# First mixture: weights split ahead of the branch, weight buffers taken in another order, rows by one queue

## The chip, the cores and the metric

The kernel runs on one core of a Trainium2 chip. The metric is the device time of one execution in microseconds; lower is better.

## The reference, cut to what matters

Causal attention with 64-row blocks, then a mixture in which a row goes to at most one of eight experts (the first mixture), then a mixture in which every row goes through all four experts (the second). The change lies in the first mixture.

```python
def _moe_ref(x, w_skip, w_gate, w1, w2):          # N, D, E, F = 2304, 512, 8, 1024
    do_compute = x @ w_skip > 0
    out = x.copy()
    xc = x[do_compute]
    logits = xc @ w_gate
    e_idx = np.argmax(logits, axis=1)
    # gate_w: the softmax weight of the chosen expert
    for e in range(E):
        mask = e_idx == e
        h = np.maximum(xc[mask] @ w1[e], 0.0)
        y[mask] = gate_w[mask, None] * (h @ w2[e])
    out[do_compute] = xc + y
```

With the inputs of the run 807 of 2304 rows go to an expert: 7, 9, 127, 179, 459, 16, 2 and 8 rows for experts 0 to 7.

## The kernel before, in words

**Stages.** Attention is computed in tiles of at most 128 query rows; each finished tile x is stored to the array XN and, once its expert is known, scattered by POOL into a second array XS, in which every expert has a region of its own (`route`, L480). `counts` (L491) then works out how many tiles each expert needs. `m1` (L848) is the first mixture, `m2` (L1141) the second; `m2` reads XN, which `m1` has updated in place.

**The first mixture** goes through its experts in four pairs, 0 and 1, 2 and 3, 4 and 5, 6 and 7; here they are pairs 0 to 3. A pair has two parts.

1. `m1_pair` (L790) handles the first 32 rows of both experts. Its matmuls take the weights in float32 as they were loaded: `hb` (x times w1, L807), a transpose `tb` (L799), `yb` (h times w2, L823). Those rows are in one tile xa, loaded from XS once (L864).
2. Rows beyond 32 are done in tiles of 128 rows, `more` and `m1_tile`, nested conditionals at L914: tile t of a pair runs if `alls[i] > t`. These tiles use weights split into a high and a low part, `wh` and `wl` (`w_split`, L699: a copy on ACT, a subtraction on DVE). `turnb` tells at which tile the pair's second expert begins; its split is inside a conditional at L933 (L927 where the first expert has no tile). In this run pair 1 has three tiles (one of expert 2, two of expert 3), pair 2 has four (all of expert 4), pairs 0 and 3 have none.

In pairs 1 to 3 two of the first expert's eight pieces are split ahead of the conditional, by `cut` within `m1_pair`; the other six are split inside the first tile, `split(0, ...)` under `tc.If(turnb[i] > 0)` at L924.

**The weights** come from memory in pieces of 512 KB, eight per expert (four of w1, then four of w2 once both w1 are in), 16 per pair, 64 in all, plus four first pieces of the second mixture. The list `plan` (consts, L136) fixes their order; here they are loads 0 to 67. Loads 0 to 15 belong to pair 0, 16 to 31 to pair 1, 32 to 47 to pair 2; pair 3 has 48 to 56 and 61 to 67, and loads 57 to 60 are the second mixture's.

Every load goes into a buffer (a room): 7 of kind s, 4 of kind d, 8 of kind r, 2 of kind e, 21 in all; `RM` (L64) gives a kind for each load, and rooms of a kind are taken in turn. `fetch` (L780) issues loads on SP's queue as far as the room's former holder belongs to a pair whose code has been written; it is called during attention's end, twice at the start of `m1` and after each pair. SP works its queue in order, so a load that has to wait for its room holds all loads behind it. SP takes no part in the conditionals; a room whose last reader stands inside a conditional is free for SP when the engines have passed that conditional.

At the start of `m1`, SP issues loads 11 to 14, then half of xa, then loads 15 to 20; ACT issues the other half of xa. `alls` and `turnb` are read into registers (L889, L890) after the first transposes of xa. `hint` (L883) tells PE, ACT and DVE ahead of time which way the branch at L914 will go; it stands behind `m1_x` in `m1_pair`.

```python
            if k not in self.rooms or len(past) >= room and past[-room] >= self.done1:
                return
```

Of the kernel before, what the change touches and what calls it, by code (L numbers as in the profile page):

```python
# [6 lines left out]
F32 = mybir.dt.float32  # L7
# [47 lines left out]
class Kernel:  # L55
# [2 lines left out]
    PTB = 1  # L58
    TLAG = 2
    RB = 7  # L60
    R3 = 4, 8, 2
    FL = 3
    RM = "s" * 7 + "r" + "d" * 4 + "r" * 7 + "e" * 2 + "s" * 4 + "d" * 4 + "s" * 3 + "r" * 8 + "e" + "d" * 3 + "e" + "s" * 7 \
        + "r" * 4 + "e" + "d" * 4 + "r" * 4 + "e" + "s" * 2  # L64
    CM = 6
    XO = 0
    S0 = "Aa02Bb13...V.vXx"
# [50 lines left out]
    def consts(self, cp, ac):  # L118
        nc, self.cp = self.nc, cp
        self.ident = cp.tile([128, 128], F32, name="ident")  # L120
        make_identity(nc, self.ident)
        self.minus = cp.tile([128, 128], F32, name="minus")

        self.maskl = ac.tile([128, 128], F32R, name="maskl")
        self.maskr = ac.tile([128, 64], F32R, name="maskr")
        nc.vector.memset(self.maskl.bitcast(F32), 0.0)
        nc.vector.memset(self.maskr.bitcast(F32), 1.0)
        self.mask4 = ac.tile([128, 128], F32R, name="mask4")
        nc.vector.memset(self.mask4.bitcast(F32), 0.0)
# [9 lines left out]
        self.plan = [(*x, k) for x, k in zip(plan[:57] + first + plan[57:], self.RM)]  # L139
        self.size = dict(s=self.RB, d=self.R3[0], r=self.R3[1], e=self.R3[2])  # L140
        self.raws, self.done1, self.stored = {}, 0, 0
        self.rooms, self.held = dict(s=self.ws), {k: [] for k in self.size}
# [347 lines left out]
    def counts(self):  # L490
# [7 lines left out]
        V.tensor_copy(self.own, t)  # L498
        V.tensor_copy(n, self.own)
        nA, nB = (n.rearrange("p (i o) -> p i o", o=2)[:, :, o] for o in range(2))  # L500
        V.tensor_tensor(t[:, 0:4], nA, nB, ALU.add)
        V.tensor_copy(self.alls, t[:, 0:4])
        V.tensor_scalar(end, tot[:, 0:8], -128.0, 0.0, ALU.add, ALU.max)
# [179 lines left out]

        return self.ws.tile([128, 20 * D], F32, tag="raw", name=name)[:, 0:n]

    def w_raw(self, w, i, e, c, pool=None):

        cols = slice(c * 256, (c + 1) * 256)
        r = pool.tile([128, 1024], F32, tag="raw", name=f"r{i + 1}") if pool else self.raw(1024, f"r{i + 1}")
# [91 lines left out]
    def fetch(self, n=99):  # L781

        for _ in range(min(n, len(self.plan) - len(self.raws))):
            p, x, k = self.plan[len(self.raws)]
            past, room = self.held[k], self.size[k]
            if k not in self.rooms or len(past) >= room and past[-room] >= self.done1:
                return
            past.append(p)
            self.raws[x[0] is self.w21 or x[0] is self.w22, *x[1:]] = self.w_raw(*x, pool=None if k == "s" else self.rooms[k])

    def m1_pair(self, xT, raws, cut, x, room, hint, before):

# [3 lines left out]
        def turn(i):  # L796
            tp = self.ps_t.tile([128, 2, 128], F32, tag="t", name="tb")
            for c in range(2):
                nc.tensor.transpose(tp[:, c], hs[i][:, c * 128:(c + 1) * 128], self.ident)  # L799
            hT.append(wk.tile([128, 2, 128], F32, tag=f"hT{i}", bufs=1, name="hT"))  # L800
            nc.scalar.copy(hT[i], tp)

        for i, raw in enumerate(raws):
            hp = self.ps_h.tile([128, 256], F32, tag="h", name="hb")
            for k in range(4):
                for j in range(4):
                    nc.tensor.matmul(hp[32 * j:32 * j + 32], lhsT=xT[i](k),  # L807
                                     rhs=raw[2 * (j // 2) + k // 2][:, k % 2, j % 2 * 256:j % 2 * 256 + 256],
                                     start=(k == 0), stop=(k == 3))
            cut()  # L810
            hs.append(wk.tile([128, 256], F32, tag=f"hs{i}", bufs=1, name="hs"))
            nc.scalar.activation(hs[i], hp, AF.Relu)
        turn(0)
        before()
        turn(1)
        x = self.m1_x(x, room)
        hint()
        cut()
        for i, raw in enumerate(raws):
            yps.append(self.ps_y.tile([128, 512], F32, tag=f"y{i}", name="yb"))  # L820
# [6 lines left out]
    def m1_join(self, i, yps):  # L827
# [7 lines left out]
        def out():  # L835
            p = slice(0, 64)
            x = self.xa[:, i]
            sm = self.ps_t.tile([128, 512], F32, tag="t", name="ysum")
            for o in range(2):
                nc.tensor.matmul(sm[32 * o:32 * o + 32], lhsT=self.sel, rhs=ys[o], start=True, stop=True)  # L840
            y = wk.tile([128, 512], F32, tag="sy", bufs=1, name="ys")
            nc.vector.scalar_tensor_tensor(y[p], sm[p], x[:, DM + 1:RW], x[:, 0:DM], ALU.mult, ALU.add)
            nc.gpsimd.indirect_dma_start(out=self.XN, out_offset=bass.IndirectOffsetOnAxis(
                ap=x[:, DM:DM + 1].bitcast(I32), axis=0), in_=y[p], in_offset=None, bounds_check=N - 1, oob_is_err=False)
        return out

    def m1(self):
# [10 lines left out]
            at = nc.values_load(self.row[0:1, i, t:t + 1], engines=pool, min_val=2 * i * N, max_val=2 * i * N + 2 * N - 128)  # L858
            return self.m1_load(bass.ds(at, 128), "xq", 2, nc.gpsimd, xg=xg)

        self.fetch(4)
        for i, q in enumerate((nc.sync, nc.scalar)):
            self.scat = list(scat)
            self.m1_load(None, q=q, xg=self.xa[ROWS * i:ROWS * i + ROWS], src=XE[i::2, 0:ROWS, :].rearrange("e n w -> n e w"))  # L864
        self.scat = list(scat)
        xs = [load(0, 0)]
        self.fetch()
# [21 lines left out]
        alls = [nc.values_load(self.alls[0:1, i:i + 1], engines=en + pool, min_val=0, max_val=TM) for i in range(E1 // 2)]  # L889
        turnb = [nc.values_load(self.turnb[0:1, i:i + 1], engines=both, min_val=0, max_val=99 + TM) for i in range(E1 // 2)]  # L890
        for i in range(E1 // 2):
            es = 2 * i, 2 * i + 1
            raws = [[self.raws[False, h, e, c] for h in range(2) for c in range(4)] for e in es]
# [18 lines left out]
            def more(t, x, y):  # L912

                with tc.If(alls[i] > t, label=f"pair{i}_{t}"):  # L914
                    last = t + 1 == TM
                    z = None if t + 2 >= TM else load(i, t + 2, xi[(t + 2) % 3])
                    at = [0]
# [12 lines left out]
                    y, put = self.m1_tile(x, ws, sp, mid=lambda: None if last else self.m1_x(y, ix[(t + 1) % 2]),  # L930
                                          late=self.YL[t > 0], hint=lambda: None if last else hint(i, t + 1))
# [320 lines left out]
    def build(self):  # L1252
# [5 lines left out]
        with contextlib.ExitStack() as top:  # L1258
# [8 lines left out]
            with contextlib.ExitStack() as st:  # L1267
# [12 lines left out]
                def scored():  # L1280

                    early.close()
                    self.wd = self.rooms["d"] = opener(top)("wd", self.R3[0], side="right")
                    self.rooms["r"] = opener(first)("wr", self.R3[1], side="right")

                self.attention(scored)
            with contextlib.ExitStack() as st:
                en = opener(st)
                self.wp = en("wb", 1)
                self.rooms["e"] = en("we", self.R3[2])  # L1290
# [60 lines left out]
```

## Time and profile before

| what | value |
|---|---|
| median of 3 runs | 1174.28 us (1172.23 to 1175.66) |
| profiled execution | 1174.58 us, span 1172.9 us |
| PE busy | 1088.8 us, 93% of the span |
| attention and routing | 0 to about 223 us |
| first mixture | about 223 to 398 us |
| second mixture | about 398 us to the end |

The profile is one execution. Engine times are busy times; the granted clock of TensorE (PE) is given as a share of full speed, 1.00 for 2.4 GHz and 0.50 for 1.2 GHz. DMA share is the mean busy share of 16 DMA engines (it can read a little over 1). A name that ends in q (SPq, DVEq) is the engine's sequencer, which issues transfers, waits and branches.

### The profile page before, as it was taken

What the parts mean: (1) busy time and instruction counts of PE and PEld (TensorE: products, weight loads), DVE (VectorE), ACT (ScalarE), POOL (GpSimd) and SP (SyncE); (2) the same over time, 40 slices, a digit from 0 to 9 for tenths busy, and PEclk for the clock granted to TensorE, in tenths of its full rate; (3) what the DMA queues carried; (4) which work ended last, traced back from release to release, by engine and by line L of the source; (5) the groups of instructions that cost most, each with busy time, mean ns of one, the idle gap of its engine ahead of it and who ended that gap; (6) DMA issues with size and microseconds to landing.
All of it is one profiled execution on the core that took longest, in us unless ns stands there. A gap on an engine that the chain in (4) does not pass through costs nothing.

```text
span 1172.9 us, 19153 instructions
## 1 busy us (share of the span) xinstructions
PE 1088.8 (93%) x7359; PEld 922.5 (79%) x7359; DVE 717.9 (61%) x1171; ACT 488.7 (42%) x826; POOL 561.4 (48%) x588
## 2 busy tenths in 40 slices
PE   5888988389997799999999999999999999999998
PEld 4788878347584388999898888988888888888887
DVE  6778676455522564666666666666746767676665
ACT  5897875255412444232233323333453323233331
POOL 7988883201111134445444544445465555554551
PEclk8999989699998899999999999999999999999999
DMA  5998949994616511111111111111411111111101
GB/s 191 201 225 214 184 115 253 304 358 157 223 38 234 198 63 36 36 37 55 36 37 37 37 47 43 37 51 46 137 56 54 54 54 54 55 53 54 38 1 72
DMA packets 117562, 122.39 MB, mean 104 GB/s; under 512 B 62893, under 2 KB 79277, under 8 KB 117440
## 3 DMA queue, kind: packets, MB, share of 16 engines
q1 hardware_dynamic: 113904, 112.87, 33.7%
q0 software_dynamic: 3392, 7.73, 1.9%
q8 instruction: 64, 1.05, 0.4%
q14 instruction: 58, 0.48, 0.1%
q10 hardware_dynamic: 144, 0.26, 0.1%
HBM read 91.04 MB, written 18.64 MB: 94 GB/s over the span
## 4 chain that ended last, share of the span: by engine, by line
PE 62%; DMA 5%; issue 4%; DVE 2%; ACT 1%; POOL 1%; POOLq 0%; SPq 0%; ACTq 0%; DVEq 0%
PE yp L708 11%; PE yp L707 11%; PE yp L709 11%; PE hp L708 10%; PE hp L709 9%; PE hp L707 9%; DMA XN<-ys,xi 3%; DMA XN<-ys,xa 1%; DVE acc L1133 0%; DMA x<-XN 0%; DVE xsl L982 0%; ACT hh L1078 0%; PE hb L807 0%; DVE C L1071 0%; POOL C L1071 0%
## 5 line engine op out<-in xcount | busy, mean ns | idle before, releaser
L1133 DVE SCALAR_TENSOR_TENSOR acc<-yp,p,acc 128x512 f32<-128x512 f32 x270 | 199.1, 746 | 110.2 <-PE yp L709 110.2
L708 PE MATMUL yp<-vl,hh 128*128 128x512 f32 x576 | 226.8, 394 | 2.1 <-POOL vl L1048 2.1
L1078 ACT ACTIVATE hh<-C 128x512 fp32r<-128x512 f32 (+2 forms) x98 | 81.7, 834 | 350.6 <-DVE C L1071 305.3
L707 PE MATMUL yp<-vh,hh 128*128 128x512 f32 x576 | 225.8, 392 | 0.9 <-DVE xs L979 0.8
L709 PE MATMUL yp<-vh,hl 128*128 128x512 f32 x576 | 225.4, 391 | 0.0
L1079 DVE SCALAR_TENSOR_TENSOR hl<-C,hh 128x512 fp32r<-128x512 f32 (+2 forms) x98 | 93.8, 957 | 99.7 <-ACT hh L1078 99.7
L1071 POOL TENSOR_TENSOR p<-C,p 128x256 f32<-128x256 f32 (+2 forms) x49 | 49.6, 1012 | 210.2 <-ACT p L1068 210.2
L709 PEld LDWEIGHTS yp<-vh,hl 128*128 128x128 f32 x576 | 108.4, 188 | 23.4
L708 PEld LDWEIGHTS yp<-vl,hh 128*128 128x128 f32 x576 | 108.7, 189 | 19.5 <-POOL vl L1048 2.8
L707 PEld LDWEIGHTS yp<-vh,hh 128*128 128x128 f32 x576 | 108.7, 189 | 19.1 <-DVE xs L979 1.6
L1048 POOL TENSOR_TENSOR vl<-r,vh 128x512 fp32r<-128x512 f32 x60 | 77.7, 1307 | 75.2 <-ACT vh L1042 75.2
L1071 DVE TENSOR_TENSOR C<-hp,p 128x256 f32<-128x256 f32 (+2 forms) x147 | 80.1, 545 | 50.8 <-PE hp L709 26.3
L708 PE MATMUL hp<-xsl,th 128*128 128x256 f32 (+2 forms) x294 | 98.8, 336 | 0.7 <-DVE xsl L982 0.7
L707 PE MATMUL hp<-xsh,th 128*128 128x256 f32 (+2 forms) x294 | 98.8, 336 | 0.0
L709 PE MATMUL hp<-xsh,tl 128*128 128x256 f32 (+2 forms) x294 | 98.4, 335 | 0.0
L300 ACT ACTIVATE E<-s,m 128x320 f32<-128x320 f32 (+4 forms) x160 | 75.6, 531 | 14.7 <-DVE m L293 12.6
L1071 POOL TENSOR_TENSOR C<-C 128x256 f32<-128x256 f32 (+2 forms) x49 | 52.7, 1076 | 49.0 <-ACT C L1068 47.1
L333 POOL TENSOR_TENSOR HL<-E,HL 128x1152 bf16<-128x1152 f32 (+2 forms) x37 | 63.6, 1730 | 21.9 <-ACT HL L332 19.1
L293 DVE TENSOR_REDUCE m<-s 128x1 f32<-128x576 f32 (+3 forms) x80 | 64.5, 817 | 14.8 <-PE s L284 14.0
L708 PE MATMUL hp<-xdl,dh 128*128 128x256 f32 (+2 forms) x196 | 65.8, 336 | 0.5 <-DVE xdl L972 0.5
L707 PE MATMUL hp<-xdh,dh 128*128 128x256 f32 (+2 forms) x196 | 65.8, 336 | 0.0
L709 PE MATMUL hp<-xdh,dl 128*128 128x256 f32 (+2 forms) x196 | 65.6, 335 | 0.0
(248 smaller groups left out, 2574.9 us busy)
## 6 DMA issues: line engine op xcount, KB each, us to landing
r<-in_w_dram SPq DMA_DIRECT2D x128, 512.0 KB, 5.4
XN<-x SPq DMA_DIRECT2D x18, 256.0 KB, 5.1
vr<-in_v_dram SPq DMA_DIRECT2D x7, 640.0 KB, 7.7
out_dram<-acc SPq DMA_DIRECT2D x16, 256.0 KB, 2.0
qr<-in_q_dram SPq DMA_DIRECT2D x7, 576.0 KB, 5.4
kr<-in_k_dram SPq DMA_DIRECT2D x7, 576.0 KB, 7.0
x<-XN SPq DMA_DIRECT2D x6, 512.0 KB, 3.7
xi<-XS POOLq DMA_DIRECT2D x11, 257.0 KB, 4.5
```

The source lines that it names most:

```text
L293: nc.vector.tensor_reduce(mo, mi, axis=ax, op=ALU.max, negate=True)
L300: nc.scalar.activation(e, views[j], AF.Exp, bias=m[:R, c:c + 1])
L333: (nc.vector if item[:2] in self.HV else nc.gpsimd).tensor_tensor(HL[:R, w:2 * w].bitcast(BF16), Et[:R, 0:w], HL[:R, 0:w], ALU.subtract)
L707: nc.tensor.matmul(out, lhsT=ah, rhs=bh, start=start, stop=False)
L708: nc.tensor.matmul(out, lhsT=ah, rhs=bl, start=False, stop=False)
L709: nc.tensor.matmul(out, lhsT=al, rhs=bh, start=False, stop=stop)
L1048: nc.gpsimd.tensor_tensor(vl[:, f], r2[:, f], vh[:, f].bitcast(F32), ALU.subtract)
L1071: add = lambda e, o, x, y: e.tensor_tensor(o, x, y, ALU.add)
L1078: nc.scalar.activation(hh, C[:, i:i + 2], AF.Relu)
L1079: V.scalar_tensor_tensor(hl, C[:, i:i + 2], 0.0, hh.bitcast(F32), ALU.max, ALU.subtract)
L1133: nc.vector.scalar_tensor_tensor(a, yp, self.p[:, n, e:e + 1], a, ALU.mult, ALU.add)
```

## The change

What it does:

- **Split ahead.** In pairs 1 and 2 all eight pieces of the first expert are split by `cut` in `m1_pair`, ahead of the conditional (`todo` is now a list per pair); the six pieces follow the transposes, ahead of `yb`. In pair 3 two stand ahead and six in the first tile, as before, without the inner conditional. The branch for a first expert without tiles is gone: `counts` gives that expert one tile if the second has any.
- **Rooms.** There are 22 (e has three). Rooms of kinds r and e are named one by one (r0 to r7, e0 to e2) and `RM` picks each; the second mixture's four pieces stand one place later in `plan` (loads 58 to 61), so pair 3 has loads 48 to 57 and 62 to 67.
- **Rows.** xa comes in four transfers, all on SP's queue (pairs 0 and 1 first), ahead of any load of `m1`: `fetch(4)` is gone.
- **Registers.** `alls` and `turnb` are read before those transfers.
- **Hint.** It is called between the two experts' `hb` matmuls.
- **Buffers.** `hs` and `hT` share the buffers of the tiles' `hi` and `lo`; the pair's result `sy` shares that of the tiles' `syi`.

```diff
-    R3 = 4, 8, 2
+    R3 = 4, 8, 3
...
+        V.tensor_scalar(t[:, 4:8], nB, 1.0, None, ALU.min)
+        V.tensor_tensor(nA, nA, t[:, 4:8], ALU.max)
...
         for i, raw in enumerate(raws):
+            if i:
+                hint()
...
         x = self.m1_x(x, room)
-        hint()
         cut()
...
-            y = wk.tile([128, 512], F32, tag="sy", bufs=1, name="ys")
+            y = wk.tile([128, 512], F32, tag="syi", bufs=1, name="ys")
...
-        self.fetch(4)
-        for i, q in enumerate((nc.sync, nc.scalar)):
-            self.scat = list(scat)
-            self.m1_load(None, q=q, xg=self.xa[ROWS * i:ROWS * i + ROWS], src=XE[i::2, 0:ROWS, :].rearrange("e n w -> n e w"))
+        alls = [nc.values_load(self.alls[0:1, i:i + 1], engines=en + pool, min_val=0, max_val=TM) for i in range(E1 // 2)]
+        turnb = [nc.values_load(self.turnb[0:1, i:i + 1], engines=both, min_val=0, max_val=99 + TM) for i in range(E1 // 2)]
+        for i in range(2):
+            for o in range(2):
+                self.m1_load(None, q=nc.sync, xg=self.xa[ROWS * o:ROWS * o + ROWS, 2 * i:2 * i + 2],
+                             src=XE[4 * i + o:4 * i + 4:2, 0:ROWS, :].rearrange("e n w -> n e w"))
...
-            early = 2 if i else 8
-            todo = [(0, 1), (1, 1)] if i else [(2, 2), (4, 1), (5, 3)]
+            todo = [[(2, 2), (4, 1), (5, 3)], [(0, 1), (1, 1), (2, 6)], [(0, 1), (1, 1), (2, 6)], [(0, 1), (1, 1)]][i]
...
                     def sp(n):
-                        k, at[0] = at[0], at[0] + 1
-                        if not t:
-                            m, n = ((2, 5), (7, 1), (8, 0))[k]
-                            if n and m >= early:
-                                with tc.If(turnb[i] > 0):
-                                    split(0, m, n)
-                            if not k:
-                                with tc.If(turnb[i] == 0):
-                                    split(1, 0, 8)
+                        if todo:
+                            split(0, *todo.pop(0))
```

The first place is ACT's order around pair 2's conditional. `wh<-r` is the copy of a split, `hs<-hb` follows the two `hb` of the pair, `xih` is the first tile's x, and L914 (L917 in the change) is the conditional. Before:

```order
L812 ACTIVATE hs<-hb 128x256
L801 COPY hT<-tb 128x256 x2
L723 CAST xih<-tp 128x512
L883 REGISTER_ALU
L1347 BRANCH_PREFETCH_HINT
L914 COMPARE_AND_BRANCH
L924 COMPARE_AND_BRANCH
L701 CAST wh<-r_6968 128x1024
L701 CAST wh<-r_6970 128x1024
L701 CAST wh<-r_9414 128x1024
```

And of the change:

```order
L817 ACTIVATE hs<-hb 128x256
L804 COPY hT<-tb 128x256 x2
L725 CAST xih<-tp 128x512
L703 CAST wh<-r_6955 128x1024
L703 CAST wh<-r_6957 128x1024
L703 CAST wh<-r_9382 128x1024
L703 CAST wh<-r_9384 128x1024
L703 CAST wh<-r_9386 128x1024
L703 CAST wh<-r_9388 128x1024
L917 COMPARE_AND_BRANCH
```

Six copies have moved from behind the conditional to ahead of it, and the inner conditional L924 is gone; DVE's subtractions stand likewise.

The second place is SP's queue at the start of `m1`; r1 are pieces of w1, r2 of w2, and r2_4189 is load 10. Before:

```order
L695 DMA r2_4189<-in_w12_dram 128x2x512
L695 DMA r2_4343<-in_w12_dram 128x2x512
L695 DMA r2_4345<-in_w12_dram 128x2x512
L695 DMA r2_4347<-in_w12_dram 128x2x512
L695 DMA r2_4349<-in_w12_dram 128x2x512
L713 DMA xa_4342<-XS_62 32x4x514
L695 DMA r2_4365<-in_w12_dram 128x2x512
```

And of the change:

```order
L697 DMA r2_4189<-in_w12_dram 128x2x512
L715 DMA xa_4344<-XS_62 32x2x514 x4
L697 DMA r2_4457<-in_w12_dram 128x2x512
L697 DMA r2_4459<-in_w12_dram 128x2x512
L697 DMA r2_4461<-in_w12_dram 128x2x512
L697 DMA r2_4463<-in_w12_dram 128x2x512
```

Loads 11 to 14 have moved behind xa's rows, which are four transfers now.

## Rows read from the trace of the kernel before

**Rows 1.** The page: the span, and busy time of each engine.

```profile
span 1172.9 us, 19153 instructions
...
PE 1088.8 (93%) x7359; PEld 922.5 (79%) x7359; DVE 717.9 (61%) x1171; ACT 488.7 (42%) x826; POOL 561.4 (48%) x588
```

**Rows 2.** Windows: stretch, its length, busy us per engine, granted clock, DMA share, GB/s.

```profile
231.20:242.70 11.50, 11.50 (x112) 5.07 (x112) 6.14 (x6) 8.14 (x12) 0.00 (x0) 0.78 1.05 388
242.70:259.00 16.30, 13.13 (x111) 5.49 (x109) 9.84 (x10) 9.80 (x14) 2.57 (x4) 0.90 0.96 332
259.00:299.10 40.10, 37.90 (x181) 30.34 (x181) 19.63 (x23) 17.39 (x25) 3.15 (x4) 1.00 0.45 164
299.10:311.90 12.80, 11.49 (x109) 4.68 (x109) 9.51 (x10) 9.41 (x14) 2.39 (x4) 1.00 0.88 307
311.90:361.80 49.90, 49.72 (x240) 40.52 (x240) 12.09 (x18) 12.43 (x21) 6.47 (x8) 1.00 0.24 84
361.80:390.60 28.80, 19.66 (x108) 5.80 (x108) 4.61 (x5) 5.05 (x9) 2.51 (x3) 0.82 0.79 281
390.60:402.10 11.50, 6.57 (x27) 4.39 (x27) 8.18 (x15) 6.72 (x11) 2.80 (x1) 1.00 0.25 69
...
425.00:1172.90 747.90, 741.19 (x3741) 643.62 (x3739) 472.50 (x672) 246.28 (x394) 367.76 (x363) 1.00 0.16 48
```

**Rows 3.** Waits of SP's queue, 205 to 405 us: total us, times, longest.

```profile
SPq L695 <- DVEq L914: 90.2, 3, 54.9
```

**Rows 4.** Waits of PE, 217 to 405 us.

```profile
PE tx L874 <- DMA xa<-XS: 11.1, 1, 11.1
PE yb L823 <- DMA r<-in_w_dram: 5.6, 9, 2.1
PE hb L807 <- DMA r<-in_w_dram: 4.7, 2, 3.4
PE hb L807 <- PEq L914: 3.9, 3, 2.8
...
PE hp L749 <- DVEq L927: 1.0, 1, 1.0
```

**Rows 5.** Timeline of SP's queue, 361 to 378 us: start, length, transfers.

```profile
362.74 14.83 SPq L695 DMA_DIRECT2D r<-in_w_dram  x14
```

**Rows 6.** Timeline of PE in pair 3: start, length, work, idle before it.

```profile
368.02 1.07 PE L807 MATMUL hb<-r,xT 128*32 128x256 f32 x16 [3.38 <-DMA r<-in_w_dram]
...
388.65 1.90 PE L823 MATMUL yb<-r,hT 128*32 128x512 f32 x10 [0.25 <-DMA r<-in_w_dram]
```

**Rows 7.** Windows in which loads run one after another, and at m2's start.

```profile
368.00:384.00 16.00, 12.05 (x55) 3.59 (x56) 1.44 (x2) 1.71 (x4) 1.49 (x2) 0.68 1.05 386
...
404.00:412.00 8.00, 6.81 (x28) 5.80 (x27) 6.15 (x12) 4.19 (x7) 2.82 (x4) 0.50 1.06 372
```

**Rows 8.** DMA issues at 217 us: transfer, size, us from issue to landing.

```profile
XS<-x,sl POOLq DMA_INDIRECT x1, 5.2
```

**Rows 9.** DMA issues at 338 us.

```profile
XN<-ys,xi POOLq DMA_INDIRECT x1, 2.7
```

**Rows 10.** The lines of a split: ns min, median, max of one.

```profile
L702 DVE TENSOR_TENSOR wl<-r,wh x34: 1215/1219/1227, 224.8 to 365.6; 128x1024 fp32r<-128x1024 f32 x34
...
L701 ACT CAST wh<-r x34: 1036/1045/1061, 223.7 to 364.6; 128x1024 fp32r<-128x1024 f32 x34
```

**Rows 11.** Timeline of POOL, 360 to 396 us.

```profile
362.81 1.02 POOL L778 DMA_INDIRECT XN<-ys,xi  x1 [8.40 <-DVEq L914]
372.67 0.55 POOL L713 DMA_DIRECT2D xi<-XS  x1 [8.84 <-PE hb L807]
375.86 0.94 POOL L843 DMA_INDIRECT XN<-ys,xa  x1 [2.63 <-DVE ys L842]
393.97 2.80 POOL L843 DMA_INDIRECT XN<-ys,xa  x1 [17.17 <-DVE ys L842]
```

More of the change, by code (lines that the diff above doesn't have):

```diff
@@ L60 @@
     RB = 7
-    R3 = 4, 8, 2
+    R3 = 4, 8, 3
     FL = 3
-    RM = "s" * 7 + "r" + "d" * 4 + "r" * 7 + "e" * 2 + "s" * 4 + "d" * 4 + "s" * 3 + "r" * 8 + "e" + "d" * 3 + "e" + "s" * 7 \
-        + "r" * 4 + "e" + "d" * 4 + "r" * 4 + "e" + "s" * 2
+    RM = ("s " * 7 + "r0 " + "d " * 4 + "r1 r2 r3 r4 r5 r6 r7 e0 e1 e2 " + "s " * 4 + "d " * 4 + "s " * 3
+          + "r0 r1 r2 r3 r4 r5 r6 r7 e0 d d e1 e2 " + "s " * 7 + "r0 r1 r2 e0 r7 d d d d r3 r4 r5 r6 e1 e2").split()
     CM = 6
@@ L138, in consts @@
         first = [(E1 // 2, (w, i, 0, c)) for c in range(2) for i, w in enumerate((self.w21, self.w22))]
-        self.plan = [(*x, k) for x, k in zip(plan[:57] + first + plan[57:], self.RM)]
-        self.size = dict(s=self.RB, d=self.R3[0], r=self.R3[1], e=self.R3[2])
+        self.plan = [(*x, k) for x, k in zip(plan[:58] + first + plan[58:], self.RM)]
+        self.size = dict(s=self.RB, d=self.R3[0])
         self.raws, self.done1, self.stored = {}, 0, 0
-        self.rooms, self.held = dict(s=self.ws), {k: [] for k in self.size}
+        self.rooms, self.held = dict(s=self.ws), {k: [] for k in self.RM}
         self.hist = ac.tile([128, E1 + 1], BF16, name="hist")
@@ L684, in raw, with w_raw @@
         return self.ws.tile([128, 20 * D], F32, tag="raw", name=name)[:, 0:n]
-    def w_raw(self, w, i, e, c, pool=None):
+    def w_raw(self, w, i, e, c, pool=None, tag="raw"):
         cols = slice(c * 256, (c + 1) * 256)
-        r = pool.tile([128, 1024], F32, tag="raw", name=f"r{i + 1}") if pool else self.raw(1024, f"r{i + 1}")
+        r = pool.tile([128, 1024], F32, tag=tag, name=f"r{i + 1}") if pool else self.raw(1024, f"r{i + 1}")
         if w is self.w11:
@@ L784, in fetch @@
             p, x, k = self.plan[len(self.raws)]
-            past, room = self.held[k], self.size[k]
-            if k not in self.rooms or len(past) >= room and past[-room] >= self.done1:
+            past, room = self.held[k], self.size.get(k, 1)
+            if k[0] not in self.rooms or len(past) >= room and past[-room] >= self.done1:
                 return
             past.append(p)
-            self.raws[x[0] is self.w21 or x[0] is self.w22, *x[1:]] = self.w_raw(*x, pool=None if k == "s" else self.rooms[k])
+            self.raws[x[0] is self.w21 or x[0] is self.w22, *x[1:]] = self.w_raw(*x, pool=None if k == "s" else self.rooms[k[0]],
+                                                                                               tag="raw" if k == "d" else k)
     def m1_pair(self, xT, raws, cut, x, room, hint, before):
@@ L798, in turn @@
             for c in range(2):
-                nc.tensor.transpose(tp[:, c], hs[i][:, c * 128:(c + 1) * 128], self.ident)
-            hT.append(wk.tile([128, 2, 128], F32, tag=f"hT{i}", bufs=1, name="hT"))
+                nc.tensor.transpose(tp[:, c], hs[i][:, c], self.ident)
+            hT.append(wk.tile([128, 4, 128], F32R, tag="hlo", name="hT").bitcast(F32)[:, 0:2])
             nc.scalar.copy(hT[i], tp)
         for i, raw in enumerate(raws):
+            if i:
+                hint()
             hp = self.ps_h.tile([128, 256], F32, tag="h", name="hb")
@@ L810, in m1_pair @@
             cut()
-            hs.append(wk.tile([128, 256], F32, tag=f"hs{i}", bufs=1, name="hs"))
-            nc.scalar.activation(hs[i], hp, AF.Relu)
+            hs.append(wk.tile([128, 4, 128], F32R, tag="hhi", name="hs").bitcast(F32)[:, 0:2])
+            nc.scalar.activation(hs[i], hp.rearrange("p (c f) -> p c f", c=2), AF.Relu)
         turn(0)
@@ L888, in m1 @@
         turn(0)
-        alls = [nc.values_load(self.alls[0:1, i:i + 1], engines=en + pool, min_val=0, max_val=TM) for i in range(E1 // 2)]
-        turnb = [nc.values_load(self.turnb[0:1, i:i + 1], engines=both, min_val=0, max_val=99 + TM) for i in range(E1 // 2)]
         for i in range(E1 // 2):
@@ L916, in more @@
                     z = None if t + 2 >= TM else load(i, t + 2, xi[(t + 2) % 3])
-                    at = [0]
+                    todo = [(2, 5), (7, 1)] if i == 3 and not t else []
                     def sp(n):
-                        k, at[0] = at[0], at[0] + 1
-                        if not t:
-                            m, n = ((2, 5), (7, 1), (8, 0))[k]
-                            if n and m >= early:
-                                with tc.If(turnb[i] > 0):
-                                    split(0, m, n)
-                            if not k:
-                                with tc.If(turnb[i] == 0):
-                                    split(1, 0, 8)
+                        if todo:
+                            split(0, *todo.pop(0))
                     y, put = self.m1_tile(x, ws, sp, mid=lambda: None if last else self.m1_x(y, ix[(t + 1) % 2]),
@@ L1283, in scored @@
                     self.wd = self.rooms["d"] = opener(top)("wd", self.R3[0], side="right")
-                    self.rooms["r"] = opener(first)("wr", self.R3[1], side="right")
+                    self.rooms["r"] = opener(first)("wr", 1, side="right")
                 self.attention(scored)
@@ L1289, in build @@
                 self.wp = en("wb", 1)
-                self.rooms["e"] = en("we", self.R3[2])
+                self.rooms["e"] = en("we", 1)
                 self.wk, self.wx = en("wk", 2), en("wx", 2)
```

## The prediction

> **What bounds the kernel now.** The page comes first: TensorE (PE) is busy 93% of 1172.9 us [rows 1], but that is a mean. The table of windows is cut at the places where PE begins something new [rows 2]. From 425 us on PE is busy 741.2 of 747.9 us, at full clock and with the DMA engines at 0.16. That stretch cannot be moved by transfers, and the change does not touch it; it only begins sooner or later. What is to be won lies before it, in the four pairs of the first mixture. Each pair opens with a part that computes from the raw weights: 11.5 us in pair 0 (231.2 to 242.7), 16.3 in pair 1, 12.8 in pair 2, 28.8 in pair 3. The work is the same four times, so pair 3 spends some 16 us on something else. The table shows what: in pair 2's tiles, just before, the DMA share is 0.24, in pair 3's opening 0.79.
>
> The waits say why. SP's queue of weight loads stood 90.2 us in three waits for DVE's branch at L914, 54.9 us in one [rows 3]. The timeline of SP shows the end of the longest: at 362.74 us, right behind pair 2's last tile, 14 loads are issued in one go [rows 5]. So pair 3 starts with 6 of its 16 pieces, and PE waits for the others: 4.7 us at `hb`, 5.6 us at `yb` in all pairs [rows 4], the last wait ending at 388.65 us [rows 6]. The rest of the 28.8 us is the same work at a granted clock of 0.82 on average [rows 2].
>
> **Pair 3, the term that decides.** SP holds load 54 because its room is read last by the split inside pair 2's conditional. With the change that split stands ahead of the conditional, so the rooms of pair 2's first expert are free some 50 us before the tiles end: one copy takes 1.05 us and one subtraction 1.22 [rows 10], six of them about 7 us on DVE. Loads 48 to 61 can then come during the tiles, where 49.9 us at a DMA share of 0.24 have room for them. Only six, 62 to 67, go into rooms of the second expert and still wait for the branch.
>
> How long is pair 3's opening with six late loads? Pair 2 is the nearest row: there four loads wait for the same branch and PE needs them for its last `yb`; the opening takes 12.8 us. A load alone on the engines takes 524 KB / 386 GB/s = 1.36 us [rows 7]. Two more make 12.8 + 2 x 1.36 = 15.5 us. Against 28.8 that is **-13.3 us**. The bounds: in pair 3 the first load after the branch reached PE at 368.02 - 362.74 = 5.3 us [rows 5, 6]; with five more at 1.36 and the last 1.90 us of `yb` it is 14.0 us, and with the 0.9 us from the tiles' end to the first issue 14.9 (-13.9). If POOL's row transfers take the engines for two loads' time, it is 18.2 (-10.6). If loads no longer bound it at all, it is pair 0's 11.5 (-17.3).
>
> **The start and pair 1.** Here the change costs something. In pair 1's opening the DMA share is 0.96 and in pair 0's 1.05 [rows 2]: the weights, not PE, set when pair 1's tiles begin. Four loads (11 to 14) used to run while the last scatters were on their way, and now stand behind xa: 4 x 1.36 = +5.4 us for every load that follows. In return the last scatter, 5.2 us from issue to landing while loads fill the engines [rows 8], should take about as long as one on idle engines, 2.7 us [rows 9]: -2.5. With 22 rooms one load fewer waits for pair 0's branch, and the idle share in 242.7 to 259 can be filled: (1.05 - 0.96) / 1.05 x 16.3 = -1.4. Sum for the last load of pair 1: +1.5. The first tile of pair 1 no longer waits for the inner conditional: -1.0 [rows 4]. Net **+0.5 us**. Bounds: +4.4 if only the 1.0 comes back; -2.4 if, besides, the four loads find half of their time in other gaps.
>
> Several parts end in this same wait for weights and count nothing: xa's rows sooner (PE waited 11.1 us for them), registers read during that wait, and the hint sooner, which is to shorten the 3.9 us in which PE waited for code at three branches, 2.8 in the longest [rows 4]. All three let pair 0 finish sooner, and pair 1 then waits longer for its loads. If that cover were gone, they would be worth up to the 2.8 us and some 2 us of the wait for xa. Four transfers for two add two issues on SP, under a microsecond, into the same cover. The two added operations of `counts` work on 128x4 numbers behind the wait for the scatter.
>
> Pair 2 keeps its opening: its last four loads wait for pair 1's branch as before, **0**. Six splits now stand ahead of its conditional, 6 x 1.05 = 6.3 us on ACT, while PE is at `yb` for longer than that; the tile uses the two oldest pieces first. The shared `syi` makes the pair's result wait until the previous tile's scatter has landed; what stands behind it on DVE is the first tile's x and six subtractions, 7.3 us, against the 12.8 of the opening: **0**, at worst 2.
>
> **The clock.** After stretches in which PE waits for weights the granted clock is at the lower of its two levels, 1.2 GHz: 0.68 on average in 368 to 384 us, 0.50 in 404 to 412 [rows 7]. Pair 1 will wait more than before, so its first tile could start at the lower level; 8 us at 0.50 cost 4. In pair 2 and at the end of pair 3, with the same pattern of late loads, the clock was 1.00 [rows 2], and I take **0**. The Trainium skill, "TensorE: Matmul & The Clock Gate", section on oscillation in real kernels, says that bursts of matmuls with waits for DMA between them each start cold. By that rule the sum would carry the 4 us; the rows bear it out in pair 3 and not in pair 2, so it is a rival below.
>
> **The sum.** -13.3 + 0.5 + 0 = -12.8. The profiled execution took 1174.58 us, 0.3 over the median 1174.28, so the profile would read 1161.8 and the median **1161.5 us**.
>
> **Rivals.**
> - *Cold tiles.* Pair 1 is starved for longer and its first tile runs at the lower clock: +4, 1165.5. For it: 404 to 412 us. Against: 311.9 us on, 1.00 right behind late loads. Chance 0.12.
> - *POOL becomes the bound of pair 3.* POOL must end pair 2's scatters before it passes pair 3's branch; its scatter of the last tile is issued at 362.81, the next row load at 372.67, the pair's scatter at 375.86 and the last one at 393.97 [rows 11]. If the first three keep their distance from the tiles' end (361.8), the third lands, at some 6 us, 20 us behind it; the last scatter would be wanted at 15.5 + 3.4 = 19 us. With POOL's way to the branch, some 3 us more: +4, 1165.5. Against: with 6 loads in flight for 14 they land sooner. Chance 0.08.
> - *Pair 1 is not bound by loads.* Then the start gives its gains: about -4 more, 1157.5. The DMA share of 1.05 speaks against it. Chance 0.06.
> - *The room is not free ahead of the branch.* If SP's wait still ends only where the conditional is left, the change does not do what it says: pair 3 keeps its 28.8 us, and the four loads moved behind xa cost pair 1 their 4.4. That ends slower, at 1178.7. It decides if load 54 is issued behind pair 2's last tile. For it: all three long waits of SP ended at a branch [rows 3]. Against: the order of ACT shows the six copies ahead of the branch, with nothing inside it that reads those rooms. Chance 0.03.
>
> **How the numbers follow.** My forecast has 0.71. Its own bounds (-10.6 to -13.9 in pair 3, -2.4 to +4.4 in pair 1) and the first two rivals put eight of ten cases into 1156.5 to 1167. About 0.3% (3.5 us) is what a measurement of this kernel can tell from no change. Faster by more than that: all cases but the last, less a small part in which two rivals and a bound meet, 0.94. Within it 0.03, slower 0.03.
>
> **What would show it.** Right: SP's longest wait for DVE's branch falls from 54.9 to at most 90.2 - 54.9 = 35.3 us, what its two other waits make together; in pair 2's tiles the DMA share rises from 0.24 to over 0.5; behind pair 2's last tile only six loads are issued; pair 3's opening takes 14 to 18 us and `hb` there waits for nothing. The wait for xa falls from 11.1 to 6 to 8 us, and pair 1's `yb` waits for weights more than before, its tiles starting within 4 us of 260. Wrong: pair 3's opening over 20 us, pair 1's tiles starting at 265 or later, or a granted clock under 0.9 in pair 1's tiles.

## The result and the profile after

| | before | change |
|---|---|---|
| median of 7 runs | 1173.95 us (1168.59 to 1175.66) | 1163.34 us (1156.92 to 1164.99) |
| ratio | | 0.9913, 95% interval 0.9884 to 0.9941 |
| profiled execution, span | 1174.58, 1172.9 | 1164.91, 1163.3 |

The change is faster by 10.6 us; 1161.5 was forecast, between 1156.5 and 1167. Two later comparisons of the same kernel gave 0.9911 (0.988 to 0.9941) and 0.9880 (0.9859 to 0.9901).

The page of the change, the lines of [rows 1]:

```profile
span 1163.3 us, 19119 instructions
PE 1085.5 (93%) x7359; PEld 919.6 (79%) x7359; DVE 719.9 (62%) x1173; ACT 489.1 (42%) x826; POOL 564.8 (49%) x588
```

Windows of the change, cut where [rows 2] is cut: the openings of pairs 0 and 1, pair 1's tiles, pair 2's opening and tiles, pair 3's opening.

```profile
229.80:241.60 11.80, 11.75 (x112) 5.03 (x112) 8.01 (x8) 8.14 (x12) 0.00 (x0) 0.83 1.04 379
241.60:265.60 24.00, 17.30 (x110) 4.68 (x109) 11.52 (x11) 10.72 (x15) 2.58 (x4) 0.93 1.05 390
265.60:303.90 38.30, 37.63 (x181) 30.40 (x180) 16.61 (x19) 16.13 (x23) 3.15 (x4) 1.00 0.42 152
303.90:317.20 13.30, 11.40 (x109) 4.54 (x109) 6.33 (x7) 10.64 (x15) 1.76 (x3) 1.00 0.86 300
317.20:366.70 49.50, 49.49 (x241) 40.65 (x240) 15.50 (x20) 11.51 (x20) 10.69 (x9) 1.00 0.47 168
366.70:382.20 15.50, 13.37 (x108) 4.69 (x108) 4.54 (x5) 4.97 (x9) 2.50 (x3) 1.00 0.74 250
```

One cut of [rows 2] lay half a microsecond late: pair 1's tiles ended at 298.6 there, not at 299.1, so that they took 39.6 us and pair 2's opening 13.3. These two windows of the kernel before:

```profile
259.00:298.60 39.60, 37.90 (x181) 30.34 (x180) 19.15 (x22) 17.06 (x24) 3.15 (x4) 1.00 0.46 166
298.60:311.90 13.30, 11.49 (x109) 4.68 (x109) 9.99 (x10) 9.74 (x14) 2.39 (x4) 1.00 0.85 296
```

The issue of the last scatter into XS is a good zero for the start. The timeline of POOL has it at 217.48 us in the kernel before and at 221.09 in the change:

```profile
217.48 0.97 POOL L480 DMA_INDIRECT XS<-x,sl  x1 [1.06 <-issue]
```

```profile
221.09 0.98 POOL L480 DMA_INDIRECT XS<-x,sl  x1 [0.67 <-POOL x L469]
```

With it the whole span divides as follows.

| stretch | before | change | difference |
|---|---|---|---|
| to the last scatter's issue | 217.5 | 221.1 | +3.6 |
| from there to pair 1's first tile | 41.5 | 44.5 | +3.0 |
| pair 1's tiles | 39.6 | 38.3 | -1.3 |
| pair 2's opening | 13.3 | 13.3 | 0 |
| pair 2's tiles | 49.9 | 49.5 | -0.4 |
| pair 3's opening | 28.8 | 15.5 | -13.3 |
| the rest | 782.3 | 781.1 | -1.2 |
| sum | 1172.9 | 1163.3 | -9.6 |

The waits of SP's queue and of PE in the change, against [rows 3] and [rows 4]:

```profile
SPq L697 <- DVEq L917: 74.2, 2, 39.1
...
SPq L715 <- DVE row L521: 1.0, 1, 1.0
```

```profile
PE tx L880 <- DMA xa<-XS: 7.4, 1, 7.4
PE yb L827 <- DMA r<-in_w_dram: 4.9, 9, 1.4
...
PE hb L812 <- DMA r<-in_w_dram: 3.0, 5, 2.0
PE hb L812 <- PEq L917: 2.7, 3, 1.6
```

And SP's timeline behind pair 2's last tile, against the 14 loads of [rows 5]:

```profile
367.60 4.98 SPq L697 DMA_DIRECT2D r<-in_w_dram  x6
```

So six loads are late in pair 3, where 14 were (the second mixture's four among them). Its opening ends 13.3 us sooner and runs at full clock throughout (0.82 before), and pair 2's tiles carry the loads now: a DMA share of 0.47 for 0.24. Against that stands the start: pair 1's opening takes 24.0 us instead of 16.3, with the DMA engines at 1.05 throughout.

### The profile page after: what moved, and what is told of

It is laid out like the page before. It is cut to its first block, busy times and chain, and to the rows that moved or that the text cites. A ratio compares the mean times of both kernels' runs of the same rounds, so it can differ in the third digit from the quotient of the medians.

```text
span 1163.3 us, 19119 instructions
## 1 busy us (share of the span) xinstructions
PE 1085.5 (93%) x7359; PEld 919.6 (79%) x7359; DVE 719.9 (62%) x1173; ACT 489.1 (42%) x826; POOL 564.8 (49%) x588
## 4 chain that ended last, share of the span: by engine, by line
PE 62%; DMA 7%; issue 5%; DVE 2%; ACT 1%; POOL 1%; POOLq 0%; DVEq 0%; SPq 0%; ACTq 0%
PE yp L710 11%; PE yp L709 11%; PE yp L711 11%; PE hp L710 10%; PE hp L711 10%; PE hp L709 9%; DMA XN<-ys,xi 4%; DMA XN<-ys,xa 2%; DMA XN<-ys,xg 1%; DVE acc L1129 0%; DVE xsl L978 0%; ACT hh L1074 0%; DMA x<-XN 0%; DVE C L1067 0%; PE tp L960 0%
## 5 line engine op out<-in xcount | busy, mean ns | idle before, releaser
L300 ACT ACTIVATE E<-s,m 128x320 f32<-128x320 f32 (+4 forms) x160 | 75.6, 531 | 17.7 <-DVE m L293 15.6
L333 POOL TENSOR_TENSOR HL<-E,HL 128x1152 bf16<-128x1152 f32 (+2 forms) x37 | 63.2, 1717 | 25.2 <-ACT HL L332 22.5
```

The source lines that it names most:

```text
L300: nc.scalar.activation(e, views[j], AF.Exp, bias=m[:R, c:c + 1])
L333: (nc.vector if item[:2] in self.HV else nc.gpsimd).tensor_tensor(HL[:R, w:2 * w].bitcast(BF16), Et[:R, 0:w], HL[:R, 0:w], ALU.subtract)
```

## The experiments

All compare with the kernel before on the same chip. The stretches are those of the table.

**The change once more.** No edit.

> The changed kernel once more, unaltered. The issue of the last scatter into XS stood at 217.5 us in the profile of before and at 221.1 in that of the change, though nothing of the change runs so early. Theory (attention's end varies from run to run): the issue falls anywhere from 217 to 221 us, and the stretches behind it repeat within 0.5 us: 44.5 us from that issue to the first tile of pair 1 (before: 41.5), 15.5 us from the end of pair 2's tiles to the end of pair 3's yb. Rival (the change itself makes attention longer): the issue again at 221 us.

Measured: 1165.83 us for 1177.15, 0.9911 (0.988 to 0.9941). The last scatter is issued at 220.9 us, pair 1's first tile starts 44.6 us behind it; pair 3's opening takes 15.5. The stretches behind the scatter repeat within 0.2 us. On the attention's end this run alone fits the rival; other profiles speak against it. The split ahead alone, below, has the code of before up to there and issues its last scatter at 226.0 us, 8.5 later than the profile of before; the change with both gains has it at 218.2; the ten profiles of the experiments lie between 218.2 and 229.2. The 3.6 us of the first line of the table lie well inside this spread, and no run shows that they are the work of the change. What sets the attention's end in a run was not tried.

**The split back in the tile.** In pairs 1 and 2 the first expert's six later pieces are split in the first tile, in an inner conditional; everything else is the change.

```diff
-            todo = [[(2, 2), (4, 1), (5, 3)], [(0, 1), (1, 1), (2, 6)], [(0, 1), (1, 1), (2, 6)], [(0, 1), (1, 1)]][i]
+            todo = [[(2, 2), (4, 1), (5, 3)], [(0, 1), (1, 1)], [(0, 1), (1, 1)], [(0, 1), (1, 1)]][i]
-                    todo = [(2, 5), (7, 1)] if i == 3 and not t else []
+                    todo = [(2, 5), (7, 1)] if i and not t else []
                         if todo:
-                            split(0, *todo.pop(0))
+                            with tc.If(turnb[i] > 0):
+                                split(0, *todo.pop(0))
```

> The changed kernel with the split ahead undone: in pairs 1 and 2 the first expert's six later pieces are split inside the first tile again, in an inner conditional; rooms, start and hint stay as in the change. First theory (as predicted: the place of the split frees the rooms): SP holds load 54 until pair 2's tiles end, pair 3's opening goes back from 15.5 to about 28 us, 1175 us in all. Rival (which load's room is taken decides): by the waits in the program load 54 gets the room of load 34 and waits only for a split in the first tile of pair 2; pair 3's opening stays at 15 to 16 us, the time within 2 us of the changed kernel's.

Measured: 1166.25 us, 0.9928 (0.99 to 0.9955). Pair 2's tiles and pair 3's opening:

```profile
319.60:369.10 49.50, 49.50 (x241) 40.65 (x240) 14.22 (x19) 12.43 (x21) 8.66 (x8) 1.00 0.47 170
369.10:384.70 15.60, 13.25 (x109) 4.70 (x108) 4.54 (x5) 4.96 (x9) 2.50 (x3) 1.00 0.72 248
```

SP behind the last tile:

```profile
370.05 4.04 SPq L697 DMA_DIRECT2D r<-in_w_dram  x6
```

And SP at the start of the tiles, loads 54 to 61:

```profile
317.72 13.12 SPq L697 DMA_DIRECT2D r<-in_w_dram  x8
```

The first theory falls. The split stands inside the conditional again, and all loads up to 61 are issued by 330.8 us, 38 us ahead of the tiles' end; 15.6 us for pair 3's opening, as in the change. A load may wait for a split in the first tile, which is done early in 50 us. What costs is a wait for the second expert's split, which stands in conditionals up to the last tile. By the addresses in the program, load 54 of the kernel before takes the room of load 39, a piece of pair 2's *second* expert; with the rooms named it takes that of load 34, a piece of the first. So rooms of a kind without names are not simply taken in turn, as the description of the kernel before has it, and the conditional that SP has to see passed is the one nearest around the room's last reader.

**The split ahead alone.** The kernel before, with all eight pieces split ahead in pairs 1 and 2.

```diff
-            early = 2 if i else 8
-            todo = [(0, 1), (1, 1)] if i else [(2, 2), (4, 1), (5, 3)]
+            early = 2 if i == 3 else 8
+            todo = [[(2, 2), (4, 1), (5, 3)], [(0, 1), (1, 1), (2, 6)], [(0, 1), (1, 1), (2, 6)], [(0, 1), (1, 1)]][i]
```

> The kernel before with one part of the change: in pairs 1 and 2 all eight pieces of the first expert are split ahead of the conditional; 21 rooms by kind, start, registers and hint as before. First theory (the place of the split): seven loads are late in pair 3 instead of fourteen, its opening takes 15.5 + 1.36 = 16.9 us instead of 28.8; from the last scatter's issue to pair 1's first tile about 41 us as before; in all some 12 us faster than before, 1162 us. Rival (only naming the rooms frees them): 28.8 us again, and the time of before.

Measured: 1168.93 us, 0.9931 (0.9909 to 0.9954), 8.2 us faster than before where 12 were expected. Its stretches show the 12 us; the rest is open (its profiled execution, at 1169.18 us, had the late scatter of 226.0 us, which says nothing of the other nine). The stretches are as expected: 41.5 us to pair 1's first tile, and pair 3's opening:

```profile
370.10:387.00 16.90, 14.29 (x109) 4.83 (x108) 4.63 (x5) 5.01 (x9) 2.51 (x3) 1.00 0.75 261
```

```profile
371.05 5.15 SPq L695 DMA_DIRECT2D r<-in_w_dram  x7
```

Seven late loads, 16.9 us. The rival falls too: without named rooms the split ahead is enough, and by the addresses load 54 takes load 34's room here as well. So each of the two edits, the split ahead and the table of named rooms, does it without the other, and the change does it twice. The start alone, below, does not: load 54 takes load 39's room there. Why the choice among unnamed rooms follows the place of the splits was not tried; that it does, the two programs show.

**The start alone.** The kernel before with xa in four transfers by SP, ahead of loads 11 to 14, and the registers ahead of them.

```diff
-        self.fetch(4)
-        for i, q in enumerate((nc.sync, nc.scalar)):
-            self.scat = list(scat)
-            self.m1_load(None, q=q, xg=self.xa[ROWS * i:ROWS * i + ROWS], src=XE[i::2, 0:ROWS, :].rearrange("e n w -> n e w"))
+        alls = [nc.values_load(self.alls[0:1, i:i + 1], engines=en + pool, min_val=0, max_val=TM) for i in range(E1 // 2)]
+        turnb = [nc.values_load(self.turnb[0:1, i:i + 1], engines=both, min_val=0, max_val=99 + TM) for i in range(E1 // 2)]
+        for i in range(2):
+            for o in range(2):
+                self.m1_load(None, q=nc.sync, xg=self.xa[ROWS * o:ROWS * o + ROWS, 2 * i:2 * i + 2],
+                             src=XE[4 * i + o:4 * i + 4:2, 0:ROWS, :].rearrange("e n w -> n e w"))
```

> The kernel before with another part alone: xa's rows in four transfers by SP ahead of loads 11 to 14, and the registers read ahead of them; splits, rooms and hint as before. Theory (the four loads behind xa cost pair 1): from the last scatter's issue to pair 1's first tile 44 to 46 us instead of 41.5, the last scatter lands in about 2.3 us instead of 5.2, pair 3's opening stays at about 28.8, in all 3 to 4 us slower than before. Rival (the start is neutral and something else, the 22nd room or the hint, delays pair 1): 41 to 42 us and the time of before.

Measured: 1179.32 us, 1.0025 (1.0004 to 1.0045), 2.2 us slower than before where 3 to 4 were expected. The last scatter lands in 2.2 us, and pair 1's first tile follows 44.4 us behind its issue. Pair 3's opening is long as before:

```profile
365.60:394.90 29.30, 19.54 (x109) 5.52 (x108) 4.64 (x5) 5.02 (x9) 2.51 (x3) 0.83 0.78 276
```

The start loses 2.9 us by itself, and pair 1's tiles, which begin later, take 1.2 less (38.4 us for 39.6). It has 21 rooms and the old hint and loses as much as the change does with 22 and the new one: these two bring nothing in that stretch.

**Four loads ahead of xa again, and two.** The change, with one line more ahead of xa's transfers.

```diff
+        self.fetch(4)
         for i in range(2):
             for o in range(2):
```

> The changed kernel with loads 11 to 14 issued ahead of xa's rows again (all else as in the change). Theory (pair 1 is bound by the loads, and the four behind xa are what the new start cost): from the last scatter's issue to pair 1's first tile 41.5 us as in the kernel before, instead of 44.5; the last scatter takes about 5 us again instead of 2.3; in all 3 us faster than the changed kernel, about 1160 us where that one has 1163. Rival (the scatter that lands sooner pays for the four loads): 44 to 45 us and the changed kernel's time.

The other has `self.fetch(2)` there.

> The same with only two of the four loads ahead of xa's rows. The DMA engines stand idle for about 5 us while the last scatter is on its way; two loads take 2.7 of it. Theory (any load moved ahead of xa brings its 1.36 us less what it delays the scatter): between the two, 42.5 to 43.5 us from the last scatter's issue to pair 1's first tile. Rival (two fit into the idle time and delay nothing): 41.5 us, with the scatter at 2.3 to 3 us, as good as four.

Measured: four 1161.35 us, 0.9853 (0.981 to 0.9896); two 1164.79, 0.9871 (0.983 to 0.9911), the before of both being 1176.91. These intervals overlap the change's own, so the stretch decides: 41.7 us with four, 41.4 with two. The last scatter by the DMA view, us to landing, first with four loads ahead, then with two; above each the busy share of the DMA engines, a digit in tenths for each of 40 slices (220.5 to 223 us, 229 to 231 us), which begin just before the scatter's issue:

```profile
DMA  9989999998999999999999899799969998999998
XS<-x,sl POOLq DMA_INDIRECT x1, 5.8
```

```profile
DMA  0000000000000000000060000000000000023310
XS<-x,sl POOLq DMA_INDIRECT x1, 2.3
```

Two loads ahead delay nothing, as the rival of the second expectation has it, but not for its reason. They do not run while the scatter is on its way: in this profile, with its late scatter, they had landed before it was issued. In the kernel with both gains, the last experiment, they run about 1.2 us into the scatter's way, and it lands in 2.6 us:

```profile
DMA  9997969999997847956252125320000000000000
XS<-x,sl POOLq DMA_INDIRECT x1, 2.6
```

(40 slices of 218 to 221 us; the scatter is issued at 218.24.) With four loads the engines are busy until about 224.5 us, almost 4 us into the scatter's way. Another two loads ahead are worth 2 x 1.36 = 2.7 us by the price of a load alone, an estimate, and cost the scatter 3.5.

**Two late loads in pair 2.** The change, with four rooms swapped.

```diff
-          + "r0 r1 r2 r3 r4 r5 r6 r7 e0 d d e1 e2 " + "s " * 7 + "r0 r1 r2 e0 r7 d d d d r3 r4 r5 r6 e1 e2").split()
+          + "r0 r1 r2 r3 r4 r5 r6 r7 e0 d d s s e1 e2 " + "s " * 5 + "r0 r1 r2 e0 r7 d d d d r3 r4 r5 r6 e1 e2").split()
```

> The changed kernel with four rooms of pair 2 renamed: loads 44 and 45 take the s rooms that loads 24 and 25 left, 46 and 47 take e1 and e2. Only two loads of pair 2 wait for pair 1's conditional instead of four. Theory (an opening takes as long as its late loads: 13.3 us with four, 14.4 with five, 15.5 with six, 16.9 with seven, so 1.2 us each, down to the 11.5 us of pair 0 where matmuls bind): pair 2's opening 11.5 to 12 us instead of 13.3, in all 1.5 us faster than the changed kernel. Rival (the late loads only hide something else, such as the row transfers or the code): 13 us or more.

Measured: 1163.25 us, 0.9859 (0.9821 to 0.9898). Pair 2's opening and tiles:

```profile
303.60:313.50 9.90, 9.36 (x109) 4.35 (x109) 3.20 (x3) 7.89 (x13) 1.02 (x1) 1.00 0.81 272
313.50:364.50 51.00, 49.92 (x244) 40.48 (x240) 18.61 (x23) 14.25 (x23) 11.40 (x10) 1.00 0.47 168
```

The opening falls to 9.9 us, below the floor that was given: pair 0's 11.5 has a granted clock of 0.78 in it, and at 1.00 the same matmuls take 9.4. The tiles take 1.5 us more, with more of the splits inside them (18.61 us of DVE for 15.50). PE waits there 0.6 us for the low part of the first tile's x from DVE and 0.4 for its rows; the change has no such wait.

**Two late loads in pair 3 as well.** The change with another table of rooms; the second mixture's first pieces come last.

```diff
-        self.plan = [(*x, k) for x, k in zip(plan[:58] + first + plan[58:], self.RM)]
+        self.plan = [(*x, k) for x, k in zip(plan + first, self.RM)]
-    RM = ("s " * 7 + "r0 " + "d " * 4 + "r1 r2 r3 r4 r5 r6 r7 e0 e1 e2 " + "s " * 4 + "d " * 4 + "s " * 3
-          + "r0 r1 r2 r3 r4 r5 r6 r7 e0 d d e1 e2 " + "s " * 7 + "r0 r1 r2 e0 r7 d d d d r3 r4 r5 r6 e1 e2").split()
+    RM = ("s " * 7 + "r0 " + "d " * 4 + "r1 r2 r3 r4 r5 r6 r7 e0 e1 e2 " + "s " * 2 + "d " * 4 + "s " * 5
+          + "r0 r1 r2 r3 r4 d d r5 r6 r7 e0 d d e1 e2 " + "s " * 7 + "r0 r1 r2 r5 r6 r7 e0 r3 r4 " + "d " * 4).split()
```

> The changed kernel with another table of rooms: in pair 2 two loads wait for pair 1's conditional, in pair 3 two instead of six wait for pair 2's; the second mixture's first four pieces come last, behind them, into the d rooms. Theory (1.2 us per late load, down to 11.5): pair 2's opening 11.5 to 12 us instead of 13.3, pair 3's 11.5 to 12.5 instead of 15.5, the second mixture's first four pieces still in time, so 14.5 us from pair 3's last yb to the second mixture's first matmuls as now; in all 5 us faster than the changed kernel. Rival (the second mixture's pieces, split earlier in the change during pair 2's tiles, now come too late): the openings shorten but that stretch grows by 2 to 4 us and the gain is 1 to 3 us.

Measured: 1164.0 us, 0.9872 (0.9839 to 0.9905); the interval overlaps the change's own, and the stretches decide. Pair 3's opening, 5.3 us shorter than in the change:

```profile
369.40:379.60 10.20, 9.64 (x108) 4.64 (x108) 3.60 (x4) 4.97 (x9) 1.02 (x1) 1.00 0.84 266
```

From its end to the second mixture's first matmuls it takes 21.4 us where the change takes 14.5. That is the rival's growth, but 6.9 us instead of 2 to 4, and for another reason. PE's and DVE's waits behind 369.4 us:

```profile
PE ysum L844 <- DVEq L917: 4.5, 1, 4.5
PE t L1003 <- DVE ys L846: 2.7, 1, 2.7
```

```profile
DVE ys L846 <- DMA xi<-XS: 7.2, 1, 7.2
DVE ys L846 <- DMA XN<-ys,xi: 4.7, 1, 4.7
```

PE does not wait for the second mixture's pieces but for the pair's result, and DVE there for row transfers. In the change the same wait of DVE, its longest there, ended with PE:

```profile
DVE ys L846 <- PE ysum L844: 6.7, 1, 6.7
```

POOL's timeline in this kernel, then in the change:

```profile
370.45 1.02 POOL L780 DMA_INDIRECT XN<-ys,xi  x1 [8.39 <-DVEq L917]
381.10 0.55 POOL L715 DMA_DIRECT2D xi<-XS  x1 [9.63 <-DVE xil L726]
382.13 0.93 POOL L847 DMA_INDIRECT XN<-ys,xa  x1 [0.48 <-DMA r<-in_w_dram]
388.73 2.80 POOL L847 DMA_INDIRECT XN<-ys,xa  x1 [5.67 <-DVE ys L846]
```

```profile
367.76 1.02 POOL L780 DMA_INDIRECT XN<-ys,xi  x1 [8.40 <-DVEq L917]
378.43 0.55 POOL L715 DMA_DIRECT2D xi<-XS  x1 [9.64 <-DVE xil L726]
379.46 0.93 POOL L847 DMA_INDIRECT XN<-ys,xa  x1 [0.48 <-DMA r<-in_w_dram]
385.58 2.80 POOL L847 DMA_INDIRECT XN<-ys,xa  x1 [5.19 <-DVE ys L846]
```

From the last tile's scatter to the mixture's last scatter it takes 18.3 us here and 17.8 in the change, though PE's opening is 5.3 us shorter here. Pair 2's opening (9.9 us for 13.3), the tiles (50.7 for 49.5), pair 3's opening and the stretch behind it add up to 0.6 us less than in the change, where 5 were expected. The first of the four takes 7.4 us to land in the change while late loads run, 2.7 where none does (the tile scatter at 343.17):

```profile
XN<-ys,xi POOLq DMA_INDIRECT x1, 7.4
...
XN<-ys,xi POOLq DMA_INDIRECT x1, 2.7
```

**Both gains.** The change with `self.fetch(2)` ahead of xa and the four rooms swapped; beside it the change itself.

> The changed kernel unaltered, beside the next one on the same chip: 0.991 of the kernel before, as in its earlier runs (0.9913 and 0.9911); 44.6 us from the last scatter's issue to pair 1's first tile, 15.5 us for pair 3's opening.

> The changed kernel with the two gains together: two loads ahead of xa's rows, and only two late loads in pair 2. Theory (they lie in different stretches and add): 41.4 us from the last scatter's issue to pair 1's first tile (-3.1), pair 2's opening 9.9 (-3.4), its tiles 51.0 (+1.5), to the second mixture 15.5 (+1.0): 4 us faster than the changed kernel, 0.987 to 0.988 of the kernel before. Rival (pair 1's tiles that start sooner only wait elsewhere, and POOL's chain takes back the rest): within 1 us of the changed kernel, 0.991.

Measured: the change 1159.31 us, 0.9880 (0.9859 to 0.9901), with 44.8 us from the scatter to pair 1's first tile and 15.3 for pair 3's opening; both gains 1154.40, 0.9833 (0.9813 to 0.9853). The intervals do not meet: 4.9 us faster than the change, 19.6 faster than before. Pair 1's tiles, pair 2's opening and tiles, pair 3's opening:

```profile
259.50:297.80 38.30, 37.62 (x181) 30.39 (x180) 16.62 (x19) 16.13 (x23) 3.15 (x4) 1.00 0.50 183
297.80:307.60 9.80, 9.28 (x108) 4.30 (x108) 3.20 (x3) 7.81 (x13) 1.02 (x1) 1.00 0.78 272
307.60:358.10 50.50, 50.01 (x244) 40.53 (x240) 18.61 (x23) 14.34 (x23) 11.41 (x10) 1.00 0.47 171
358.10:373.20 15.10, 13.72 (x109) 4.69 (x108) 4.54 (x5) 4.97 (x9) 2.50 (x3) 1.00 0.75 256
```

Pair 1's first tile follows 41.3 us behind the scatter's issue; the gains of the two stretches add.

## Why the prediction was right, and where it was not

**Pair 3, right in size, in part by luck.** -13.3 us forecast, 28.8 to 15.5 measured. Two slips of the sum cancel: the 12.8 us of pair 2 came from the late boundary in [rows 2] and should have been 13.3, and a late load costs less than the 1.36 us of [rows 7], so that 13.3 + 2 x 1.36 would have been 16.0. Counting late loads and pricing them by pair 2's opening holds across kernels: 9.9 us with two, 13.3 with four, 14.4 with five (pair 2 with the split in the tile and with the split ahead alone), 15.5 with six, 16.9 with seven. From four to seven that is 1.1 to 1.4 us a load; from two to four it is 1.7, for which no run gives the cause. At 14 late loads it gives 16.9 + 7 x 1.36 = 26.4; the other 2.4 of the 28.8 stand beside a granted clock of 0.82, and no run separates the two.

**Pair 3, wrong in cause.** The step that failed is "SP holds load 54 because its room is read last by the split inside pair 2's conditional", taken for the first expert's split, which the change moves. The room was that of a piece of the second expert; the table of named rooms frees it without the split ahead (15.6 us with the split back in the tile), and so does the split ahead without the names (16.9). That the size came out right is luck: the split ahead alone would not have helped had load 54 kept load 39's room, and both edits lead to almost the same late loads, six and seven.

**The start and pair 1, within its bounds, terms mixed.** +0.5 us forecast; measured +3.0 to the first tile and -1.3 in the tiles, +1.7 in all. (The lower bound, -2.4, comes out as -2.2 from its own terms.) The scatter's -2.5 was -2.9 (5.2 to 2.3 us). The tile's -1.0 was -1.3, but its cause stays open: the wait is gone and the tiles take 38.3 to 38.4 us also in the split back in the tile, the split alone and the start alone, each of which keeps an inner conditional there. The term for the 22nd room, -1.4, was nothing, since the start alone loses as much with 21 rooms. And one cover was gone: `counts` was to "work behind the wait for the scatter", but with the scatter landing sooner SP waits 1.0 us for its last line, `row`; the start alone, without the two added operations, has 0.7 of it. With those, 5.4 - 2.9 + 1.0 = 3.5 against the 3.0 measured.

"The weights, not PE, set when pair 1's tiles begin" was read from the DMA share; PE's own waits between 222 and 300 us show it for the change alone. Before, then the change:

```profile
PE yb L823 <- DMA r<-in_w_dram: 0.4, 2, 0.2
```

```profile
PE hb L812 <- DMA r<-in_w_dram: 3.0, 5, 2.0
PE yb L827 <- DMA r<-in_w_dram: 2.0, 3, 1.4
```

Before, PE and the loads came to the end of pair 1's opening almost together: with four loads ahead of xa in the change, where PE waits 3.0 us for loads, they bind at 41.7 us, and before has 41.5. In the change pair 0 ends 20.5 us behind the last scatter's issue instead of 25.2 (the sooner rows, registers and hint were not taken apart), and pair 1 then waits for its loads: there the prediction was right that these gains count nothing.

**Pair 2 and its splits ahead, right.** 13.3 us as before. DVE does wait 4.7 us for a scatter to land before it writes a pair's result, in the change too, and the opening hides it; with the last table of rooms, where openings take 10 us, it stands in the chain to PE's ysum. Giving the result its own buffer again was not tried.

**The clock, right.** Pair 1's tiles run at 1.00 though PE waits 5.0 us for loads in its opening: the cold tiles did not come. The Trainium skill's page "TensorE: Matmul & The Clock Gate", section on oscillation in real kernels, tells of matmul bursts that each start cold behind a DMA wait, in a kernel whose waits are longer than those ahead of pair 1's tiles. The prediction left that condition out, and pair 1's tiles do not contradict the Trainium skill there: none of PE's waits for loads in that opening is over 2.0 us. In pairs 3 and 0 the low clocks follow longer waits: 0.82 in pair 3's old opening, with 3.4 us ahead of its second group of hb, and 0.78 and 0.83 in pair 0, behind 11.1 and 7.4 us for xa.

**POOL, not yet.** 23 us were reckoned from pair 2's end to the last scatter; it is 385.58 - 366.7 = 18.9. In the change DVE's last wait there is for PE's ysum, so POOL does not bind, but the chain of POOL's row transfers and the results that wait for them is the next limit, as the last table of rooms shows.

**Signs that missed.** SP's longest wait was to fall to 35.3 us and is 39.1. The sign left out what the prediction itself says: six loads still wait for pair 2's branch, and SP stands there from 328.5 to 367.6 us, which costs only those six. The DMA share in pair 2's tiles is 0.47, not over 0.5. Pair 1's tiles start at 265.6, past the 265 that was to mean "wrong", but 3.6 us of that lie ahead of the last scatter, inside the spread of the attention's end.

**The sum.** -12.8 forecast; the stretches that the change touches give 3.0 - 1.3 - 0.4 - 13.3 = -12.0 in the profile, and the stretches ahead of them and behind them moved by +3.6 and -1.2, for which no cause is shown.

## What to carry to other kernels

When a queue works in order, ask of each held transfer whose buffer it waits for, by address and not by the code that looks guilty: moving a read and renaming a buffer may both free it, and one is enough. Count the transfers that are late behind a branch and price each at its time alone on the engines; here the number told the length of the stretch to about a microsecond, down to the compute floor at full clock. Before a transfer that must wait for a scatter, put as many loads as the engines have nearly finished when the scatter is issued (two here), and no more.

## What was not expected

- The last scatter of rows lands in 2.3 us when the two 512 KB loads ahead of it have landed, in 2.6 when they run 1.2 us into its way, and in 5.8 when four keep the engines busy for almost 4 us of it; in the first mixture a scatter takes 2.7 alone and 7.4 beside late loads.
- The end of attention, with the same work, lay anywhere from 217.5 to 229.2 us in the twelve profiles. Its cause is open; the spread is as large as the gain, so the stretches behind it have to be compared by themselves.
